# Other cuts of the expert weights and of the token rows in a routed mixture-of-experts stage

## Chip, cores, metric

One core of a Trainium2 chip. The metric is the device time of one execution in microseconds (us): 216.65 us before, the median of three (216.4 to 217.42). The profile is of one further execution with a span of 217.2 us. Times below without another source count from the start of that span.

## What is computed

An mLSTM attention cell for 4 x 8 heads, 768 steps and 40 columns gives 3,072 rows of 320 columns. A router sends each row to one of eight experts. The reference, cut to the part that the change touches:

```
logits = x @ w_gate                       # x: 3072 x 320
expert_idx = argmax(logits, axis=1)
for e in range(8):                        # rows sorted by expert
    h = maximum(x_sorted[lo:hi] @ w1[e], 0.0)     # w1[e]: 320 x 1024
    y_sorted[lo:hi] = h @ w2[e]                   # w2[e]: 1024 x 320
out = gate_w[:, None] * y_sorted[inv_perm]
```

## The kernel before

**Two stages.** Up to about 117 us the core works through 24 steps of 128 tokens: attention, then the router, then a scatter of each step's rows (`send`, L577) into a DRAM buffer sorted by expert. After that it runs the expert groups. The order on each engine is the program's order; nothing is rescheduled.

**Groups.** Each expert has three tiles of 128 rows at fixed places: a first group of two tiles and a second of one. I write (3,0) for the first group of expert 3 and (3,1) for its second. Experts 0 and 1 have their first groups done early, between the last router steps (L668 to L708). The rest run in the hand-written order L801: (2,0) (3,0) (0,1) (1,1) (4,0) (2,1) (5,0) (3,1) (4,1) (6,0) (5,1) (7,0) (6,1) (7,1). Five single tiles for experts with more than 384 rows follow. That makes 8 groups of two tiles and 13 of one, 29 tiles in all.

**One group.** `turn` (L230) transposes its rows on PE and copies the result to SBUF on DVE. The 320 columns are cut into 128, 128 and 64. The last piece is transposed twice, into partitions 0 to 63 and 64 to 127, so that two matmuls with 64 rows each can lie in the two halves of the PE array. `layer1` (L245) makes the 1,024 hidden columns in units: DVE applies the relu to the even ones (hidden columns 0 to 511), ACT to the odd ones. In a two-tile group there are four units. Units 0 and 2 each begin with four half matmuls (L258), followed by full ones (L267). In a one-tile group there are two units, and all eight half matmuls stand at the start. `layer2` (L277) multiplies by w2, ACT copies the result, and POOL scatters it to the output (L287). In PE's order the turn of the next group stands between `layer1` and `layer2` of the present one.

**Weights.** The weights lie in DRAM as 4-byte floats and are cast to 2 bytes on the way in, by DMAs that POOL issues: one of 256 rows for w1 (L178), two of 64 half rows (L183), and one for w2 (L189). An expert's weights are issued about three groups ahead. Every DMA from POOL takes the next of eight semaphores in turn and waits until the DMA eight before it has landed; POOL's later work waits behind it. L183 issues w1's last 64 rows: columns 0 to 511 to one half of the partitions, 512 to 1,023 to the other.

`warm` (L564) issues matmuls whose result nobody reads.

Of the kernel before, what the change touches and what calls it, by code (L numbers as in the profile page):

```python
# [8 lines left out]
F32 = mybir.dt.float32  # L9
BF16 = mybir.dt.bfloat16  # L10
# [9 lines left out]
def kernel(  # L20
# [13 lines left out]
    nc = tc.nc  # L34
    B, H, S, D = q.shape
    BH = B * H
    NB = S // 128
    N = B * S
    Dm = H * D
    E = moe_w_gate.shape[1]  # L40
    F = moe_w1.shape[2]
    FB = F // 128
    NT = N // 128
    PR = H // 2
    DP = 64
# [5 lines left out]
    dch = []  # L51
# [3 lines left out]
        d0 += 128  # L55
    DB = len(dch)

    FL = DB - 1
    HF = FB // 2
    wch = [d0 if dsz == 128 else Dm - 128 for d0, dsz in dch]  # L60
    assert NT * 128 == N and FB * 128 == F and D <= DP and dch[FL][1] == 64


    NJ = 3
# [5 lines left out]
    XW = 4  # L70
# [5 lines left out]
    ident_b = consts.tile([128, 128], BF16)  # L76
# [82 lines left out]
    xs = nc.dram_tensor("x_sorted", (E * NS, RW), BF16, kind="Internal").ap()  # L159

    big = ctx.enter_context(tc.tile_pool(name="big", bufs=1))
    w1_all = big.tile([128, E, FL * F + F // 2], BF16)
    w2_all = big.tile([128, E, FB, Dm], BF16)
    rte = ctx.enter_context(tc.tile_pool(name="rte", bufs=1))

# [9 lines left out]
    xg = [(x_all[:, NE * e : NE * (e + 1), :], x_all[:, NE * E + e : NE * E + e + 1, :]) for e in range(E)]  # L175

    def weights_in(e, n=1):
        nc.gpsimd.dma_start(  # L178
            w1_all[:, e, : FL * F].rearrange("p (a f) -> p a f", f=F),
            moe_w1[e, : FL * 128, :].rearrange("(a p) f -> p a f", p=128),  # L180
        )
        for i in range(2):
            nc.gpsimd.dma_start(  # L183
                w1_all[64 * i : 64 * i + 64, e, FL * F :], moe_w1[e, FL * 128 :, i * HF * 128 : (i + 1) * HF * 128],
            )

    def weights_out(e0, n):
        e = slice(e0, e0 + n)
        nc.gpsimd.dma_start(  # L189
            w2_all[:, e].rearrange("p e a d -> p (e a) d"), moe_w2[e].rearrange("e (a p) d -> p (e a) d", p=128),  # L190
        )

    def apart(ins, group):
# [24 lines left out]
    def spot(kind, shape, dtype):  # L218
        i = turns[kind] = turns.get(kind, -1) + 1
        at = spots[kind][i % len(spots[kind])]  # L220
        if isinstance(at, tuple):
            tag, pool = at
            return pool.tile(shape, dtype, name=kind, tag=tag)[:]
        n = 1
        for m in shape[1:]:
            n *= m
        at = at[:, :n]
        return at.rearrange("p (a b) -> p a b", b=shape[2]) if len(shape) == 3 else at

    def turn(g):  # L230
        n = g["n"]
        src = g["xg"] if "xg" in g else xg[g["e"]][g["k"]]
        g["xT"] = spot("xT", [128, DB, n * 128], BF16)
        tp = spot("tp", [128, DB, n * 128], BF16)
        for j in range(n):
            for db in range(DB):
                at = src[:, j, db * 128 : min(Dm, (db + 1) * 128)]
                if db < FL:
                    nc.tensor.transpose(tp[:, db, j * 128 : (j + 1) * 128], at, ident_b[:])
                    continue  # L240
                for r in range(2):
                    nc.tensor.transpose(tp[64 * r : 64 * r + 64, db, j * 128 : (j + 1) * 128], at, ident_b[:])
        nc.vector.tensor_copy(g["xT"], tp)

    def layer1(g, u):  # L245
        n = g["n"]
        per = 4 // n
        w, xT = g["w"][0], g["xT"]
        v = u // 2 * per
        if u == 0:  # L250
            g["h"] = spot("h", [128, FB, n * 128], BF16)
        if u % 2 == 0:
            g["hp"] = [spot("hp", [128, per, n * 128], F32) for _ in range(2)]
            for i in range(per):
                for a in range(2):
                    c = FL * F + (v + i) * 128
                    r = slice(64 * a, 64 * a + 64)
                    nc.tensor.matmul(  # L258
                        g["hp"][a][:, i, :], lhsT=w[r, c : c + 128], rhs=xT[r, FL, :], start=(i == 0), stop=False,
                        skip_group_check=True,  # L260
                    )
        a = u % 2
        hp = g["hp"][a]
        for i in range(per):
            for db in range(FL):
                c = db * F + (a * HF + v + i) * 128
                nc.tensor.matmul(  # L267
                    hp[:, i, :], lhsT=w[:, c : c + 128], rhs=xT[:, db, :], start=False, stop=(db == FL - 1),
                    skip_group_check=True,
                )  # L270
        dst = g["h"][:, a * HF + v : a * HF + v + per, :]
        if a == 0:
            nc.vector.tensor_relu(dst, hp)  # L273
        else:
            nc.scalar.activation(dst, hp, AF.Relu)  # L275
# [23 lines left out]
    def router():  # L299
        nc.vector.tensor_scalar_mul(wg_sb[:], wg_sb[:], -1.0)  # L300
# [6 lines left out]
    with tc.tile_pool(name="ring", bufs=1) as ring_pool, \  # L307
# [256 lines left out]
        def warm(n):  # L564
            j = ps1.tile([128, 512], F32, name="junk", tag="tk")
            for _ in range(n):
                nc.tensor.matmul(
                    j[:], lhsT=ident_b[:], rhs=st[NT - 1]["dA"][:].rearrange("p j t -> p (j t)"), start=True, stop=True,
                )

        def keep_rows(t):
            P = team_of[t]
            nc.scalar.activation(
                x_all[:, t, :Dm], st[t]["x"][:], AF.Copy, scale=rt[P]["gs"][:, t - teams[P][0] : t - teams[P][0] + 1],
            )
# [31 lines left out]
        for s in range(-3, NT):  # L607
            P, odd = (s - 4) // 2, s % 2
            last = s == NT - 1
            do(scores, s + 1)  # L610
            do(transposes, s + 2)
            if s == -3:
                masks()
            if s == -2:
                gates()
                router()
            do(values, s + 2)
            if odd and s > E and sent <= (s - 5 if s > 2 * PE_ + 4 else s - 6):
                send(sent)
                sent += 1  # L620
            if s == NT - 5:
                weights_in(0, 1)
            pair = not odd and 0 <= P
            if pair:
                gate(P)
            do(states, s)
            do(load, s + 6 if s >= -1 else -1)
            if pair:
                rank(P, s - 1)
            if last:  # L630
                warm(3)
            do(xtrans, s - 1)
            do(ogate, s + 2)
            do(attend, s)
            if pair:
                place(P)
                if P == PE_:
                    even_out(s - 1)
            if s == 2 * PE_ + 4:
                keep_rows(s - 4)  # L640
                keep_rows(s - 3)
            elif s != 2 * PE_ + 5:
# [27 lines left out]
            hp=[(t_, ps1) for t_ in ("sA", "sB", "tk", "tq")], tp=[("dC", ps1)],  # L670
            h=[kq[:, i].rearrange("p a h d -> p (a h d)").bitcast(BF16) for i in range(2)],
            xT=[kq[:, 2, a].rearrange("p h d -> p (h d)").bitcast(BF16) for a in range(2)],
# [4 lines left out]
        first, second = early  # L677
        targets(0, 0)
        turn(first)
        warm(2)  # L680
        xtrans(NT - 1)
        layer1(first, 0)
        logits(P0 + 1, NT)
# [74 lines left out]
    wk_pool = ctx.enter_context(tc.tile_pool(name="moe_wk", bufs=2))  # L758
# [24 lines left out]
        g["to"] = t[:, 0:1]  # L783

    def fetch(ex):
        wx1 = wk_pool.tile([128, FL * F + F // 2], BF16, name="wx1", bufs=XW)
        wx2 = wk_pool.tile([128, FB, Dm], BF16, name="wx2", bufs=XW)
        nc.sync.dma_start(wx1[:], w1_all[:, bass.ds(ex, 1), :].rearrange("p e b -> p (e b)"))
        nc.sync.dma_start(wx2[:].rearrange("p a b -> p (a b)"), w2_all[:, bass.ds(ex, 1)].rearrange("p e a b -> p (e a b)"))
        return wx1, wx2  # L790
# [47 lines left out]
    with tc.If(nx > XU):  # L838
        with tc.For_i(XU, nx, 1) as i:
            iv = wk_pool.tile([128, 1], F32, name="iv")  # L840
            nc.vector.tensor_copy(iv[:], invx[:, bass.ds(i, 1)])
            g = dict(n=1, w=fetch(expert_of(i)), apart=False)
# [36 lines left out]
```

## Time and profile before

| What | Value |
|---|---|
| PE busy, 145 to 167 us | 21.95 of 22 us |
| DMA engines' mean share, 117 to 178 us | 1.14 to 1.25 (transfers overlap on an engine) |
| POOL, eight weight sets: L178, L183 (each), L189 | 784, 585, 936 ns medians |
| One packet of w1, 2,048 bytes written (4,096 read) | 173 ns |
| One packet of w1, 1,024 bytes written | 96 ns |
| One packet of w2, 640 bytes written | 69 ns |

The last three rows are medians over the trace's packet records of POOL's DMA queue, where one packet is one contiguous run: 2,048, 1,024 and 8,192 packets of these sizes for eight experts. They also tell when an expert's weights were through (us from the span's start; the semaphore follows within a microsecond):

| Expert | w1 issued (POOL) | first w1 packet | last w1 packet | w1 first used | last w2 packet | w2 first used |
|---|---|---|---|---|---|---|
| 1 | 111.9 | 116.1 | 122.1 | 128.05 | 125.6 | 130.5 |
| 2 | 118.7 | 124.0 | 128.9 | 134.7 | 132.2 | 138.0 |
| 3 | 131.2 | 132.7 | 138.8 | 140.3 | 144.3 | 144.9 |
| 4 | 137.1 | 142.2 | 148.7 | 153.3 | 152.0 | 156.2 |
| 5 | 146.5 | 150.8 | 156.2 | 161.6 | 160.6 | 164.5 |
| 6 | 154.2 | 158.6 | 165.1 | 173.1 | 168.4 | 176.0 |
| 7 | 166.7 | 168.6 | 174.2 | 184.8 | 177.9 | 187.7 |

In the timeline, each line has its start, its length, the engine and source line, the operation with destination and source, a count, and in brackets how long the engine was idle before it and what ended that.

### The profile page before, as it was taken

Reading aid. Unit: us, or ns where it says so; the run is one execution under the profiler, and the core shown is the slowest. Engines: PE = TensorE matmul, PEld = TensorE weight load, DVE = VectorE, ACT = ScalarE, POOL = GpSimd, SP = SyncE. Lnnn points to the kernel's source line nnn. Section 1 sums busy time; section 2 is a strip of 40 time slices with the busy share of each in tenths; the row PEclk is TensorE's granted clock in tenths of the full one; section 3 lists DMA queues with packets and bytes.
Section 4 is the critical chain, followed back from the end, with each engine's and each line's share of the span. In section 5 each row is a group of like instructions: output and inputs, shape, how many; then the busy total and the mean of one; then the engine's idle time right before and its main releaser. Section 6 shows DMA issues by size and latency. Waiting matters only on the chain.

```text
span 217.2 us, 5727 instructions
## 1 busy us (share of the span) xinstructions
PE 192.3 (89%) x2048; PEld 151.8 (70%) x2057; DVE 124.8 (57%) x410; ACT 117.3 (54%) x273; POOL 139.3 (64%) x238
## 2 busy tenths in 40 slices
PE   1299999999999999979899998969999986999970
PEld 1168788899998899978786755647667654676740
DVE  7746667677787878797776342345833332333320
ACT  2458657797789897896751552323333322332330
POOL 6036786644869889749999489838656786253221
PEclk9999999999999999999998899999999999999996
DMA  7999999989999989994799999999999999985310
GB/s 139 197 198 190 205 205 204 231 156 254 178 193 173 195 161 206 193 204 84 142 184 262 222 205 150 193 254 233 216 229 245 231 290 408 409 317 201 149 46 10
DMA packets 120782, 44.32 MB, mean 204 GB/s; under 512 B 102506, under 2 KB 115821, under 8 KB 120752
## 3 DMA queue, kind: packets, MB, share of 16 engines
q1 hardware_dynamic: 105456, 25.34, 55.9%
q0 software_dynamic: 14832, 18.38, 40.3%
q8 instruction: 17, 0.28, 0.5%
q10 hardware_dynamic: 464, 0.21, 0.4%
q14 instruction: 13, 0.11, 0.2%
HBM read 39.30 MB, written 9.37 MB: 224 GB/s over the span
## 4 chain that ended last, share of the span: by engine, by line
PE 46%; POOL 20%; issue 14%; DVE 9%; DMA 5%; ACT 3%; POOLq 1%; ACTq 0%; DVEq 0%
POOL out_dram L287 7%; PE hp L474 6%; PE zp L280 5%; DMA w_all<-in_moe_w_dram 5%; PE hp L406 5%; PE tk L368 4%; POOL x_sorted L579 4%; PE dC L414 4%; PE hp L267 4%; PE tq L368 3%; PE xt L451 3%; PE sA L386 3%; PE sA L381 2%; POOL x_sb L444 2%; POOL rest L297 2%
## 5 line engine op out<-in xcount | busy, mean ns | idle before, releaser
L273 DVE TENSOR_SCALAR h<-hp 128x512 bf16<-128x512 f32 x25 | 17.3, 692 | 40.6 <-PE hp L267 26.3
L287 POOL DMA_INDIRECT out_dram<-zo,s_idx x20 | 20.0, 1002 | 16.3 <-ACT zo L285 10.0
L275 ACT ACTIVATE h<-hp 128x512 bf16<-128x512 f32 x25 | 14.9, 597 | 25.2 <-PE hp L267 19.9
L579 POOL DMA_INDIRECT x_sorted<-x_all,slots x24 | 25.3, 1054 | 4.9 <-issue 3.9
L444 POOL TENSOR_TENSOR x_sb<-x_sb,den 128x320 f32<-128x320 f32 x23 | 16.8, 729 | 17.2 <-DVE den L442 17.1
L280 PE MATMUL zp<-w_all,h 128*128 128x320 bf16 x160 | 24.5, 300 | 3.5 <-DMA w_all<-in_moe_w_dram 1.6
L280 PEld LDWEIGHTS <-h 128*128 128x128 bf16 x200 | 17.7, 98 | 13.2 <-DVE h L273 2.7
L285 ACT COPY zo<-zp 128x320 f32<-128x320 f32 x25 | 10.7, 426 | 27.2 <-PE zp L280 23.7
L267 PEld LDWEIGHTS <-w_all 128*128 128x128 bf16 x256 | 18.4, 98 | 5.6 <-issue 3.4
L393 ACT CAST dB<-sB 128x512 bf16<-128x512 f32 x24 | 14.0, 585 | 13.7 <-PE sB L387 11.5
L267 PE MATMUL hp<-xT,w_all 128*128 128x128 bf16 (+1 forms) x224 | 21.1, 243 | 0.0
L406 PE MATMUL hp<-C_sb,qT 104*128 104x82 f32 x160 | 20.7, 272 | 0.0
L368 PE MATMUL tk<-ident,kq 128*104 128x128 f32 x96 | 16.4, 296 | 4.2 <-DMA kq<-in_k_dram 4.2
L406 PEld LDWEIGHTS hp<-C_sb,qT 104*128 104x128 f32 x160 | 19.4, 192 | 0.3
L453 ACT COPY xT<-xt 128x384 f32<-128x384 f32 x24 | 11.6, 482 | 13.5 <-PE xt L451 12.5
L356 POOL CAST vAb<-vA 128x328 bf16<-128x328 f32 x24 | 11.0, 459 | 11.7 <-DVE vA L354 11.7
L474 PE MATMUL hp<-wg_sb,xT 128*128 128x8 f32 x144 | 18.0, 258 | 0.0
L414 PE MATMUL dC<-vA,kq 128*104 128x82 f32 x160 | 17.9, 254 | 0.0
L394 POOL TENSOR_SCALAR_AFFINE_SELECT dB<-dB 128x512 bf16<-128x512 bf16 x24 | 16.5, 689 | 1.7 <-ACT dB L393 1.5
L474 PEld LDWEIGHTS hp<-wg_sb,xT 128*128 128x128 f32 x144 | 17.4, 195 | 0.1
L391 DVE TENSOR_TENSOR dA<-sA,cmask 128x512 bf16<-128x512 f32 x24 | 16.0, 669 | 1.4 <-PE sB L387 1.4
L414 PEld LDWEIGHTS dC<-vA,kq 128*104 128x104 f32 x160 | 16.3, 172 | 0.0
(160 smaller groups left out, 455.8 us busy)
## 6 DMA issues: line engine op xcount, KB each, us to landing
wx<-w_all SPq DMA_DIRECT2D x10, 640.0 KB
w_all<-in_moe_w_dram POOLq DMA_DIRECT2D x8, 640.0 KB
w_all<-in_moe_w_dram POOLq DMA_DIRECT2D x8, 512.0 KB
kq<-in_k_dram SPq DMA_DIRECT2D x24, 160.0 KB
kq<-in_q_dram SPq DMA_DIRECT2D x24, 160.0 KB
v<-in_v_dram SPq DMA_DIRECT2D x24, 160.0 KB
o_sb<-in_o_gate_dram SPq DMA_DIRECT2D x24, 160.0 KB
x_sorted<-zrow POOLq DMA_DIRECT2D x8, 241.5 KB
```

Of the source, the lines that this page charges most:

```text
L267: nc.tensor.matmul(hp[:, i, :], lhsT=w[:, c : c + 128], rhs=xT[:, db, :], start=False, stop=(db == FL - 1), skip_group_check=True,)
L273: nc.vector.tensor_relu(dst, hp)
L280: nc.tensor.matmul(zp, lhsT=g["h"][:, fb, j * 128 : (j + 1) * 128], rhs=g["w"][1][:, fb, :], start=(fb == 0), stop=(fb == FB - 1),)
L287: ins = nc.gpsimd.indirect_dma_start(out=out[:, :], out_offset=bass.IndirectOffsetOnAxis(ap=at, axis=0), in_=zo, in_offset=None, bounds_ch ...
L368: nc.tensor.transpose(tp[:, j, :], two(d[n], j), ident[:])
L391: nc.vector.tensor_tensor(d["dA"][:], sA[:], cmask[:, None, :].to_broadcast([128, PR, 128]), op=ALU.mult)
L394: nc.gpsimd.affine_select(d["dB"][:], d["dB"][:], compare_op=ALU.is_ge, fill=0.0, base=0, pattern=[[0, PR], [1, 128]], channel_multiplier=-1,)
L406: nc.tensor.matmul(hp[:, 2 * j * D1 : (2 * j + 2) * D1], lhsT=d["qT"][:, j, :], rhs=st["C"][:, j].rearrange("p h d -> p (h d)"), start=(j ...
L414: nc.tensor.matmul(st["dC"][:, j], lhsT=two(d["k"], j), rhs=d["vA"][:, 2 * j : 2 * j + 2, :], start=(c == 0 and j == 0), stop=True, skip_g ...
L444: eng.tensor_tensor(x3d, x3d, den[:].unsqueeze(2).to_broadcast([128, H, D]), op=ALU.mult)
L474: nc.tensor.matmul(lg[:, i * E : (i + 1) * E], lhsT=st[t]["xT"][:, db * 128 : (db + 1) * 128], rhs=wg_sb[:, db, :], start=(fresh and i == ...
L579: ins = nc.gpsimd.indirect_dma_start(out=xs[:, :], out_offset=bass.IndirectOffsetOnAxis(ap=slots[:, t : t + 1], axis=0), in_=x_all[:, t, : ...
```

## The change

The 320 columns are cut into pieces that overlap: columns 0 to 127, 64 to 191, and 192 to 319. Three full transposes then give all that is needed: piece 0 holds columns 64 to 127 in its upper partitions, piece 1 the same columns in its lower ones. So one of the two 64-row halves is read from piece 1, the other from piece 0, and the two transposes of 64 columns are not needed. Hidden columns of even units take piece 0 and piece 2 in full and the other 64 columns as a half matmul; those of odd units take piece 1 and piece 2. To suit, w1's DMAs are cut anew: 128 rows of 4,096 bytes, 128 x 2 half rows, and 128 half rows.

All half matmuls of a group now stand ahead of its full ones, so a two-tile group opens four PSUM tiles at its start. In w2, two neighbouring rows go to one partition, for runs of 2,560 bytes in DRAM; the hidden columns are permuted to match, which makes the weight slices of `layer1` step over every second column. Two calls of `warm` issue two matmuls more each.

```
     def weights_in(e, n=1):
+        half = F // 2
+        at = moe_w1.offset + e * Dm * F
+        nc.gpsimd.dma_start(w1_all[:, e, :F], moe_w1[e, parts[2] : parts[2] + 128, :])
         nc.gpsimd.dma_start(
-            w1_all[:, e, : FL * F].rearrange("p (a f) -> p a f", f=F),
-            moe_w1[e, : FL * 128, :].rearrange("(a p) f -> p a f", p=128),
-        )
-        for i in range(2):
-            nc.gpsimd.dma_start(
-                w1_all[64 * i : 64 * i + 64, e, FL * F :], moe_w1[e, FL * 128 :, i * HF * 128 : (i + 1) * HF * 128],
-            )
+            w1_all[:, e, F : 2 * F].rearrange("p (a f) -> p a f", a=2),
+            bass.AP(moe_w1.tensor, at, [[F, 128], [64 * F + half, 2], [1, half]]),
+        )
+        nc.gpsimd.dma_start(
+            w1_all[:, e, 2 * F :],
+            bass.AP(moe_w1.tensor, at + half, [[128 * F - half, 2], [F, 64], [1, half]]),
+        )
...
         nc.gpsimd.dma_start(
-            w2_all[:, e].rearrange("p e a d -> p (e a) d"), moe_w2[e].rearrange("e (a p) d -> p (e a) d", p=128),
+            w2_all[:, e].rearrange("p e (a j) d -> p (e a) (j d)", j=2),
+            moe_w2[e].rearrange("e (a p j) d -> p (e a) (j d)", p=128, j=2),
         )
...
-                at = src[:, j, db * 128 : min(Dm, (db + 1) * 128)]
-                if db < FL:
-                    nc.tensor.transpose(tp[:, db, j * 128 : (j + 1) * 128], at, ident_b[:])
-                    continue
-                for r in range(2):
-                    nc.tensor.transpose(tp[64 * r : 64 * r + 64, db, j * 128 : (j + 1) * 128], at, ident_b[:])
+                nc.tensor.transpose(tp[:, db, j * 128 : (j + 1) * 128], src[:, j, parts[db] : parts[db] + 128], ident_b[:])
...
+    def column(fb):
+        return fb // 2 * 256 + fb % 2
...
-        if u % 2 == 0:
-            g["hp"] = [spot("hp", [128, per, n * 128], F32) for _ in range(2)]
-            for i in range(per):
+            g["hp"] = [spot("hp", [128, per, n * 128], F32) for _ in range(2 * n)]
+            for k in range(HF):
                 for a in range(2):
-                    c = FL * F + (v + i) * 128
-                    r = slice(64 * a, 64 * a + 64)
+                    c = 2 * F + column(k)
+                    r = slice(64 - 64 * a, 128 - 64 * a)
                     nc.tensor.matmul(
-                        g["hp"][a][:, i, :], lhsT=w[r, c : c + 128], rhs=xT[r, FL, :], start=(i == 0), stop=False,
-                        skip_group_check=True,
+                        g["hp"][k // per * 2 + a][:, k % per, :], lhsT=w[r, c : c + 255 : 2], rhs=xT[r, 1 - a, :],
+                        start=(k % per == 0), stop=False, skip_group_check=True,
                     )
...
-            for db in range(FL):
-                c = db * F + (a * HF + v + i) * 128
+            fb = a * HF + v + i
+            for c, db in ((F + column(fb), a), (column(fb), 2)):
                 nc.tensor.matmul(
-                    hp[:, i, :], lhsT=w[:, c : c + 128], rhs=xT[:, db, :], start=False, stop=(db == FL - 1),
+                    hp[:, i, :], lhsT=w[:, c : c + 255 : 2], rhs=xT[:, db, :], start=False, stop=(db == 2),
...
             if last:
-                warm(3)
+                warm(5)
...
         turn(first)
-        warm(2)
+        warm(4)
         xtrans(NT - 1)
```

More of the change, by code (lines that the diff above doesn't have):

```diff
@@ L56 @@
     DB = len(dch)
-    FL = DB - 1
     HF = FB // 2
     wch = [d0 if dsz == 128 else Dm - 128 for d0, dsz in dch]
-    assert NT * 128 == N and FB * 128 == F and D <= DP and dch[FL][1] == 64
+    assert NT * 128 == N and FB * 128 == F and D <= DP and Dm == 5 * 64
+    parts = [0, 64, 192]
     NJ = 3
@@ L161 @@
     big = ctx.enter_context(tc.tile_pool(name="big", bufs=1))
-    w1_all = big.tile([128, E, FL * F + F // 2], BF16)
+    w1_all = big.tile([128, E, 5 * F // 2], BF16)
     w2_all = big.tile([128, E, FB, Dm], BF16)
@@ L251, in layer1 @@
             g["h"] = spot("h", [128, FB, n * 128], BF16)
-        if u % 2 == 0:
-            g["hp"] = [spot("hp", [128, per, n * 128], F32) for _ in range(2)]
-            for i in range(per):
+            g["hp"] = [spot("hp", [128, per, n * 128], F32) for _ in range(2 * n)]
+            for k in range(HF):
                 for a in range(2):
-                    c = FL * F + (v + i) * 128
-                    r = slice(64 * a, 64 * a + 64)
+                    c = 2 * F + column(k)
+                    r = slice(64 - 64 * a, 128 - 64 * a)
                     nc.tensor.matmul(
-                        g["hp"][a][:, i, :], lhsT=w[r, c : c + 128], rhs=xT[r, FL, :], start=(i == 0), stop=False,
-                        skip_group_check=True,
+                        g["hp"][k // per * 2 + a][:, k % per, :], lhsT=w[r, c : c + 255 : 2], rhs=xT[r, 1 - a, :],
+                        start=(k % per == 0), stop=False, skip_group_check=True,
                     )
         a = u % 2
-        hp = g["hp"][a]
+        hp = g["hp"][u]
         for i in range(per):
-            for db in range(FL):
-                c = db * F + (a * HF + v + i) * 128
+            fb = a * HF + v + i
+            for c, db in ((F + column(fb), a), (column(fb), 2)):
                 nc.tensor.matmul(
-                    hp[:, i, :], lhsT=w[:, c : c + 128], rhs=xT[:, db, :], start=False, stop=(db == FL - 1),
+                    hp[:, i, :], lhsT=w[:, c : c + 255 : 2], rhs=xT[:, db, :], start=False, stop=(db == 2),
                     skip_group_check=True,
@@ L785, in fetch @@
     def fetch(ex):
-        wx1 = wk_pool.tile([128, FL * F + F // 2], BF16, name="wx1", bufs=XW)
+        wx1 = wk_pool.tile([128, 5 * F // 2], BF16, name="wx1", bufs=XW)
         wx2 = wk_pool.tile([128, FB, Dm], BF16, name="wx2", bufs=XW)
```

## Prediction

> **What bounds the kernel now.** I read the page's busy shares first, then the busy time by stretch, then the timeline of the expert groups, and last the packet records. The attention stage (to about 117 us) is touched by nothing but two spare matmuls. For the expert stage the stretches say which engine is full:
>
> ```profile
> 134.00:145.00 11.00, 8.67 (x78) 5.73 (x79) 5.24 (x13) 3.24 (x6) 7.02 (x9) 1.00 1.17 212
> 145.00:156.00 11.00, 10.95 (x120) 7.52 (x118) 5.89 (x19) 3.52 (x8) 7.82 (x10) 1.00 1.22 225
> 156.00:167.00 11.00, 11.00 (x111) 7.38 (x110) 4.77 (x15) 4.15 (x9) 6.39 (x8) 1.00 1.25 223
> ```
>
> The columns are length, PE, weight load, DVE, ACT, POOL, clock, DMA share, GB/s. From 145 us PE has no gap; before it there are some, and the DMA engines are full in all three. Where weights are late, the timeline says so:
>
> ```profile
> 122.12 0.53 POOL L183 DMA_DIRECT2D w_all<-in_moe_w_dram  x1 [2.11 <-DMA w_all<-in_moe_w_dram]
> ...
> 133.01 0.99 POOL L189 DMA_DIRECT2D w_all<-in_moe_w_dram  x1
> ...
> 144.86 2.33 PE L280 MATMUL zp<-w_all,h 128*128 128x320 bf16 x16 [1.64 <-DMA w_all<-in_moe_w_dram]
> 145.52 1.03 POOL L287 DMA_INDIRECT out_dram<-zo_e,s_idx  x1 [3.28 <-DMA w_all<-in_moe_w_dram]
> ```
>
> PE waits 1.64 us for w2 of expert 3, issued at 133.01. So up to 144.86 the end is set by expert 3's weights, and what PE saves earlier is lost in that wait. Later experts have 3 to 10 us in hand (table). POOL twice waits for a landing before it may issue.
>
> The price of transposes and of switching is read from one group, (2,1), with the turn of (5,0):
>
> ```profile
> 158.44 0.40 PE L258 MATMUL hp<-xT,w_all 64*128 64x128 bf16 x8
> 158.77 1.07 PE L267 MATMUL hp<-xT,w_all 128*128 128x128 bf16 x16
> 159.50 0.69 DVE L273 TENSOR_SCALAR h<-hp 128x512 bf16<-128x512 f32 x1 [1.75 <-PE hp L267]
> 159.67 0.28 PE L239 MATMUL tp<-ident_b,x_all 128*128 128x128 bf16 x2
> 159.88 0.25 PE L242 MATMUL tp<-ident_b,x_all 128*64 128x128 bf16 x2
> 160.05 0.29 PE L239 MATMUL tp<-ident_b,x_all 128*128 128x128 bf16 x2
> 160.27 0.25 PE L242 MATMUL tp<-ident_b,x_all 128*64 128x128 bf16 x2
> 160.45 1.26 PE L280 MATMUL zp<-w_all,h 128*128 128x320 bf16 x8
> ```
>
> Starts count, not durations. Sixteen full matmuls take 159.67 - 158.77 = 0.90, 0.056 each. Eight half matmuls lie in pairs, 4 x 0.056 = 0.22, but take 0.33: 0.11 is the change of shape. A tile's transposes take (160.45 - 159.67) / 2 = 0.39: three columns' worth, 0.17, and two changes of shape, 0.22.
>
> [...] No weight load of before is strided[...]; the packed ones hide behind matmuls 0.056 apart. [...]
>
> **The change part by part.**
>
> *Transposes.* Three full ones take 3 x 0.056 = 0.17 in place of 0.39: 0.22 saved per tile on PE. In a one-tile group layer2 must also wait for the first relu: 159.50 + 0.69 = 160.19, plus 0.06 to start. Before a turn of one tile nothing is gained there, since layer2 waits for DVE already; before a turn of two tiles 0.20 (160.45 to 160.25) of the 0.44.
>
> *Half matmuls first.* A two-tile group changes shape at two places rather than four: 0.22 saved in each. One-tile groups have this order already. In expert 1's early group the fourth PSUM tile is the one that ACT copies out until 128.59, while half matmuls start at 128.05: some 0.3 lost, one copy.
>
> *Sum on PE.* Before expert 3's layer2: 0.44 (turn of (2,0)), 0.66 in (2,0) (turn of (3,0) and halves), 0.22 in (3,0), less 0.1 in the early group: 1.2 us, all ahead of the weight wait. After it: two-tile groups (4,0), (5,0), (6,0), (7,0), each 0.22 and one tile's turn, 4 x 0.44; one-tile groups ahead of a two-tile turn, (1,1), (2,1), (4,1), (5,1), 4 x 0.20; the rest 0. **2.6 us** that reach the end. The last five single tiles keep their 2.99 us period, the relu being in the chain.
>
> *Spare matmuls.* In `warm(5)` two more, 0.43, fall into PE's idle 0.65 ahead of L451; `warm(4)` takes up the 0.44 that the turn ahead of it gives back. Zero; at most a better clock around 120 us (granted 0.90 from 117 to 134), under 0.5.
>
> *w2's runs.* A line through 69, 96 and 173 ns gives 19 ns + 0.075 ns per byte written, so a 1,280-byte packet 115 ns: estimate. 512 x 115 = 58.9 engine-us per expert for 1,024 x 69 = 70.7: 3.7 us per engine rather than 4.4. w1 goes from 256 x 173 + 128 x 96 = 56.6 to 128 x 173 + 384 x 96 = 59.0. POOL's issue: the same four DMAs.
>
> *Where w1's third piece runs.* Its DRAM side counts [2][64][512]; its SBUF side counts 128 partitions. [...] two engines carry 64 packets each, 64 x 96 ns = **6.1 us**, where 16 engines would take 0.8. This is the disputed cost, 0 to 5.4 us, and I take the upper end[...]. Such a pair then has per expert 8 x 0.173 + 16 x 0.096 + 6.14 = 9.1 us of w1 and 3.7 of w2, 12.8 in all, where every engine of before has 2.8 + 0.8 + 4.4 = 8.0. I expect another pair for each expert, so no engine is overloaded in total; but a weight set is there when its slowest engine is.
>
> *Following it.* Expert 1: first packet 116.1, third piece through at 125.2 to 128 rather than 122.1. The scatter of L579 at 124.47 is eight DMAs behind it and waits; the three scatters and expert 3's issue queue up on POOL. The third scatter (128.02) is eight behind w2 of expert 1, through at 129 to 132. So expert 3's weights are issued 1 to 3 us later. Expert 2's w1 is through by 133 to 134 and used at about 134: just in time. Expert 3: w1 came at full rate from 134, now from about 136, plus 9.1 us times 1.0 to 1.2 for the other traffic (before, 8.0 us of work took 10.3): **145 to 147** for a first use at about 139.5. PE idles 5 to 7 us. Then w2 on the same pair, 3.7 us: 148.5 to 151, where it was 144.3; layer1 of (3,0) fits between. I take 149: layer2 of (3,0) starts 4.2 us later than at 144.86. From there on the table's 4 us and more in hand cover the later experts, since PE is late too.
>
> **Forecast (A).** 216.65 + 4.2 - 2.6 = **218.3 us**. With the smallest delay (overlapping packets, +1.8) 215.8; with the largest (+6.5) 220.6.
>
> **Rivals.** *B: the third piece is spread over 16 engines.* For: nothing in the profile of before shows a narrow DMA. Then w2 of expert 3 comes about 0.5 us earlier (0.7 less w2, 0.15 more w1), and the end moves by 0.5 + 2.6: 213.6. *C: strided weight loads are slow.* If a load takes twice the matmul's 0.056, one-tile groups pay: 13 x 16 x 0.056 = 11.6 on full matmuls, less some 3 that waits for relu hide: about 225. Against: [...] 98 ns load records that overlap today. *D: delay and gain cancel*, PE's idle being filled by DMA engines that serve the lone pair faster: 216.6. PE's stalls of about 4 us from 176 to 183.6 ("issue") may also shift by 1 us either way.
>
> **Chances.** A 0.55 as a band from 215.8 to 221 (about a quarter of it below 215.6 to 216, a half above 217.7), B 0.30, C 0.06, D 0.09. Faster by over 0.5%: 0.28 of B and 0.13 of A, 0.41. Within: 0.13. Slower: 0.46. The range runs from B to A's upper end, 213.2 to 221.3; C and the tails are left out.
>
> **What would show it.** Right: packets of 1,024 bytes that end for each expert some 4 us after its others, with two at a time in flight at the end; PE waiting for a DMA at the first half matmuls of (3,0) for several us; POOL's scatters at 124 to 130 waiting for weight DMAs; the transposes of a tile 0.17 us apart; full matmuls of one-tile groups still 0.056 apart. Wrong: the third piece through with the rest, and POOL's timetable unmoved (B); one-tile `layer1` longer than 1.24 us (C).

## The result and the profile after

| | before | after |
|---|---|---|
| Median of four runs, us | 216.53 (215.6 to 217.42) | 222.67 (222.14 to 224.66) |
| Ratio | | 1.030, 95% interval 1.022 to 1.038 |
| Profiled execution, us (span) | 218.99 (217.2) | 223.08 (221.3) |
| layer2 of (3,0) starts | 144.86 | 153.11 |
| from there to the last scatter | 66.93 | 61.60 |
| from the last scatter to the end | 5.4 | 6.6 |

Slower, by 6.1 us. Some executions of a kernel take 1.5% or more longer than its fastest; ratios here leave those out, medians do not. The profiled execution of before, at 218.99 us, lay above all four in the median; this matters below. The three lower rows add up to the difference of the spans: 8.25 - 5.33 + 1.2 = 4.1.

Read the timeline of the changed kernel first:

```profile
128.90 1.03 POOL L580 DMA_INDIRECT x_sorted<-x_all,slots  x1 [5.79 <-ACT zo_e L286]
...
135.68 0.60 POOL L180 DMA_DIRECT2D w_all<-in_moe_w_dram  x1
...
148.78 1.03 PE L259 MATMUL hp<-xT,w_all 64*128 64x256 bf16 x8 [8.50 <-DMA w_all<-in_moe_w_dram]
149.56 1.06 POOL L288 DMA_INDIRECT out_dram<-zo_e,s_idx  x1 [4.74 <-DMA w_all<-in_moe_w_dram]
...
153.11 2.33 PE L281 MATMUL zp<-w_all,h 128*128 128x320 bf16 x16 [0.40 <-DMA w_all<-in_moe_w_dram]
```

PE stands for 8.50 us in front of the first half matmuls of (3,0). The scatter of 124.47 comes at 128.90. The trace names an ACT copy for its 5.79 us; that copy is not what ended the wait, as the experiment with only expert 1's piece narrow shows. The trace also records when a DMA's semaphore is raised, 16 times for each of these three, and these increments show both waits directly:

| Changed kernel | issued | 14 increments by | the last two | what waits for them starts |
|---|---|---|---|---|
| expert 1, third piece | 114.44 | 124.50 | 127.39, 128.07 | scatter, 128.90 |
| expert 3, third piece | 136.97 | 142.65 | 148.63, 148.74 | half matmuls of (3,0), 148.78 |
| expert 3, w2 | 137.93 | 146.97 | 152.91, 152.97 | layer2 of (3,0), 153.11 |

By stretch:

```profile
134.00:145.00 11.00, 5.45 (x54) 4.04 (x51) 2.56 (x5) 2.47 (x5) 10.14 (x15) 0.99 0.94 150
145.00:156.00 11.00, 6.81 (x57) 4.63 (x58) 2.62 (x8) 2.04 (x4) 3.83 (x5) 0.70 1.06 221
156.00:167.00 11.00, 10.75 (x124) 7.84 (x122) 7.39 (x26) 4.09 (x8) 7.46 (x10) 1.00 1.13 184
```

In the first two rows PE was busy 7.4 us less than before, 12.3 us of 22. The DMA share of the first row fell from 1.17 to 0.94: a mean over 16 engines does not show two that work for longer. The PE work itself became cheaper as planned; here are (2,1), the turn of (5,0), then (5,0):

```profile
158.31 0.40 PE L259 MATMUL hp<-xT,w_all 64*128 64x128 bf16 x8
158.64 1.07 PE L268 MATMUL hp<-xT,w_all 128*128 128x128 bf16 x16
...
159.54 0.50 PE L241 MATMUL tp<-ident_b,x_all 128*128 128x128 bf16 x6
...
160.12 1.26 PE L281 MATMUL zp<-w_all,h 128*128 128x320 bf16 x8
...
161.31 0.61 PE L259 MATMUL hp<-xT,w_all 64*128 64x256 bf16 x8
161.85 1.92 PE L268 MATMUL hp<-xT,w_all 128*128 128x256 bf16 x16
...
163.61 0.33 PE L241 MATMUL tp<-ident_b,x_all 128*128 128x128 bf16 x3
163.78 2.42 PE L281 MATMUL zp<-w_all,h 128*128 128x320 bf16 x16
```

A tile's transposes take 163.78 - 163.61 = 0.17 us. Sixteen full matmuls with weight slices that step over every second column take 159.54 - 158.64 = 0.90, as before. The narrow DMA has a signature on the page. Before, then after, from the second and third parts:

```profile
DMA packets 120782, 44.32 MB, mean 204 GB/s; under 512 B 102506, under 2 KB 115821, under 8 KB 120752
...
q0 software_dynamic: 14832, 18.38, 40.3%
```

```profile
DMA packets 124877, 44.33 MB, mean 200 GB/s; under 512 B 109674, under 2 KB 120941, under 8 KB 124848
...
q0 software_dynamic: 18928, 18.41, 40.8%
```

Same bytes, but 7,168 more packets under 512 bytes. In the packet records they are of 4 bytes and on POOL's queue (q0): 7,168 = 8 experts x 14 x 64. The number fits fourteen engines that carry nothing of a third piece and have 64 packets of 4 bytes each for it, while two carry 64 real ones; the packet records do not name the engine. For expert 3 these small packets are through by 142.3, while its real ones go on to about 148.2.

### The profile page after: what moved, and what is told of

It reads as the page before. It is cut to its first block, busy times and chain, and to the rows that moved or that the text cites. A ratio compares the mean times of both kernels' runs of the same rounds, so it can differ in the third digit from the quotient of the medians.

```text
span 221.3 us, 5677 instructions
## 1 busy us (share of the span) xinstructions
PE 187.7 (85%) x2023; PEld 152.5 (69%) x2032; DVE 123.6 (56%) x410; ACT 117.2 (53%) x273; POOL 140.7 (64%) x238
## 3 DMA queue, kind: packets, MB, share of 16 engines
q0 software_dynamic: 18928, 18.41, 40.8%
## 4 chain that ended last, share of the span: by engine, by line
PE 39%; DMA 21%; POOL 16%; DVE 8%; issue 8%; ACT 4%; SPq 1%; POOLq 0%; ACTq 0%; DVEq 0%
DMA w_all<-in_moe_w_dram 18%; PE hp L407 5%; PE hp L475 5%; PE tk L369 4%; POOL x_sorted L580 4%; PE zp L281 4%; PE dC L415 4%; POOL out_dram L288 4%; PE tq L369 3%; PE sA L387 3%; PE sA L382 3%; DMA wx<-w_all 3%; PE xt L452 3%; PE hp L268 2%; POOL x_sb L445 2%
## 5 line engine op out<-in xcount | busy, mean ns | idle before, releaser
L268 PEld LDWEIGHTS <-w_all 128*128 128x128 bf16 x256 | 19.4, 100 | 4.4 <-issue 1.9
```

The costliest lines, as they stand in the source:

```text
L268: nc.tensor.matmul(hp[:, i, :], lhsT=w[:, c : c + 255 : 2], rhs=xT[:, db, :], start=False, stop=(db == 2), skip_group_check=True,)
```

## The experiments

Five sets of kernels, each set on one chip; the third and fourth were on the same one. Before's medians there were 220.38 (the first four kernels), 223.99 (the next four), 216.86, 216.80 (four each) and 222.88 (the last two). Times are compared within a set.

**How many engines the third piece uses.** The DRAM side of that one DMA, in four versions. Two of them read other rows of w1 than the layer needs, but as many bytes; their output is not the layer's:

```
 changed:        [[128 * F - half, 2], [F, 64], [1, half]]
 four engines:   [[33 * F, 4], [F, 32], [1, half]]            # other rows of w1
 wide:           [[F, 128], [1, half]]                        # other rows of w1
 two halves:     two DMAs of 64 rows, the reference's rows
```

> The changed kernel with the third DMA's DRAM side counting 4 first, over other rows of w1 than the computation asks for, the same 128 x 2,048 bytes. Theory (engines in use follow the first count): 32 packets of 96 ns on each of four engines, 3.1 us rather than 6.1; the delay of expert 3 is between that of two engines and of sixteen: the time is 215 to 218.5 us. Rival: as with two, 221 to 223 us, or as with sixteen, 213 to 214.5 us, if engines don't follow that count.

> The changed kernel with one edit: the third DMA of w1 reads 128 rows one step apart (other rows of w1 than the computation asks for, the same 128 x 2,048 bytes), so that both of its access patterns count 128 first. Theory (third piece on two engines): the lone pair is gone; packets of 1,024 bytes end with the rest, POOL's scatter at 124 us no longer waits for a weight DMA, PE's wait of 8.5 us at the half matmuls of group (3,0) falls under 1.5 us, and the time is 213 to 214.5 us. Rival (the finer cut of w1, the four PSUM tiles opened at once or the strided weight loads cost the time): the DMA is as fine as ever, so it stays at 221 to 223 us.

> The changed kernel with w1's third piece as two DMAs of 64 rows each, as L183 had it; five DMAs per expert rather than four. Theory: 213 to 215 us, like the 128-row read, plus at most 0.6 us of POOL's issue per expert, of which only expert 3's is on the path, and a wait on the eighth DMA before that comes one DMA sooner. Rival (another part of the change costs the time): 221 to 223 us.

Four engines, in PE's timeline:

```profile
143.25 0.61 PE L259 MATMUL hp<-xT,w_all 64*128 64x256 bf16 x8 [2.90 <-DMA w_all<-in_moe_w_dram]
147.66 2.33 PE L281 MATMUL zp<-w_all,h 128*128 128x320 bf16 x16 [1.77 <-DMA w_all<-in_moe_w_dram]
```

| leading count of the third piece | 2 | 4 | 128 |
|---|---|---|---|
| packets under 512 B, more than the wide kernel's 102,506 | 7,168 = 8 x 14 x 64 | 3,072 = 8 x 12 x 32 | 0 |
| wait for weights at (3,0)'s half matmuls, us | 8.50 | 2.90 | none |
| layer2 of (3,0) starts | 153.11 | 147.66 | 143.57 |

The packet counts fit two and four engines exactly, and the wait follows. The semaphore records agree: with four engines, expert 1's third piece has twelve increments by 123.44 and four from 124.86 to 125.59. But the times missed: wide took 220.22 us (217.89 to 221.41), two halves 223.45 (219.18 to 223.62), against 220.38 (219.37 to 225.95), too scattered for a ratio; four engines 223.9, ratio 1.017 (1.013 to 1.021). The profile of the wide kernel says where its gain went, in DVE's and ACT's lines of (5,1):

```profile
179.90 0.69 DVE L274 TENSOR_SCALAR h<-hp 128x512 bf16<-128x512 f32 x1 [5.13 <-issue]
...
183.81 0.60 ACT L276 ACTIVATE h<-hp 128x512 bf16<-128x512 f32 x1 [6.56 <-remote]
```

Both engines stand still though PE's work for them is long done; PE lost 5.5 us there. PE's granted clock was then 0.50 from 181.3 to 188.1, so that layer1 of (7,0) took 3.3 us where (5,0) of the changed kernel takes 2.3. The two halves lost 6.0 us of PE in the same way, four engines 5.6. Before has such a standstill at the same group (DVE 4.54 us, PE some 3.5), the changed kernel has none.

**The same fault put into the kernel before**: its two DMAs of 64 rows merged into one whose DRAM side counts 2 first.

```
-        for i in range(2):
-            nc.gpsimd.dma_start(
-                w1_all[64 * i : 64 * i + 64, e, FL * F :], moe_w1[e, FL * 128 :, i * HF * 128 : (i + 1) * HF * 128],
-            )
+        nc.gpsimd.dma_start(
+            w1_all[:, e, FL * F :],
+            bass.AP(moe_w1.tensor, moe_w1.offset + e * Dm * F + FL * 128 * F, [[F // 2, 2], [F, 64], [1, F // 2]]),
+        )
```

> The kernel before with one edit: its two DMAs of 64 half rows become one whose DRAM side counts 2 first (three DMAs per expert rather than four, the same bytes in the same places). Theory: each expert's w1 ends on two engines with 64 packets of 96 ns each; group (3,0) waits some 6 to 10 us, the time is 221 to 226 us, with none of PE's gains. Rival (the narrow DMA is hidden): 215.5 to 217.5 us.

231.65 us, ratio 1.054 (1.049 to 1.059): one DMA fewer per expert, the same bytes, and 11 us more, above what was expected. Against before's own profile 5.9 us of it are there at layer2 of (3,0) and 1.4 at the end; where the rest goes was not followed. The narrow DMA cost as much without the new layout.

```profile
145.17 0.39 PE L258 MATMUL hp<-xT,w_all 64*128 64x256 bf16 x4 [2.02 <-DMA w_all<-in_moe_w_dram]
...
150.73 4.01 PE L280 MATMUL zp<-w_all,h 128*128 128x320 bf16 x16 [2.60 <-DMA w_all<-in_moe_w_dram]
```

**Is the standstill the work of the weight copies** for the last five tiles, which run at that time? Without them (the tiles use expert 0's weights, so their output is not the layer's), in the kernels before, changed and wide; and once with the copies kept but issued later, from ACT's queue, on top of the two halves:

```
-            groups[len(order) + x]["w"] = fetch(expert_of(x))
+            groups[len(order) + x]["w"] = (w1_all[:, 0, :], w2_all[:, 0])
```

> The kernel before without the ten copies of expert weights within SBUF for the last five single tiles, which use expert 0's weights instead (their rows come out as expert 0 would have them). Question: PE, DVE and ACT all stand still for 3 to 6 us between 175 and 188 us in each run of before and of the wide versions, just when these copies begin, and not in the changed kernel, whose copies begin 13 us later. Theory (the copies cause the standstill): it is gone, and the time falls by 3 to 5 us against before. Rival (it belongs to the scatters or to the last weights): under 1 us.

> The changed kernel without the ten copies of weights for the last five single tiles (they use expert 0's weights). Theory: in the changed kernel the copies already lay behind the groups that they disturb, so it falls by less than 1.5 us; against the kernel before without copies it is 5.5 to 7 us slower (8.3 us later at layer2 of group (3,0), less 2.6). Rival (the copies cost both the same): it falls as much as before does.

> The changed kernel with the 128-row read of other rows of w1 as third piece, and without the ten copies (the last five tiles use expert 0's weights). Theory (narrow DMA costs, the rest of the change gains, the copies hide it): 2.5 to 4 us faster than the kernel before without copies, and 8 to 10 us faster than the changed kernel without copies. Rival (PE's part of the change gains nothing): as fast as the kernel before without copies.

> The changed kernel with the third piece as two DMAs of 64 rows, and with the ten copies issued from ACT's queue in ACT's order, three groups ahead of their use, so that they begin near 185 us rather than 176. Theory (two things cost: the lone engine pair, and copies that begin among the groups): no standstill, 4 to 7 us faster than with the copies from SP, 2 to 5 us faster than the kernel before. Rival: the standstill moves along with the copies, and nothing is gained.

The late copies:

```
-        nc.sync.dma_start(wx1[:], w1_all[:, bass.ds(ex, 1), :].rearrange("p e b -> p (e b)"))
+        eng.dma_start(wx1[:], w1_all[:, bass.ds(ex, 1), :].rearrange("p e b -> p (e b)"))   # eng: ACT's queue; wx2 alike
...
-        x = i - len(order) + XW
+        x = i - len(order) + 3
```

Before without copies took 224.81 us (220.48 to 226.62) and still had the standstill, 3.9 us on PE; wide without copies had it too (PE 3.5 and 1.4). So it does not need the copies. Late copies took 225.74, ratio 1.012 (1.003 to 1.021): a miss. The pair changed and wide without copies gave 229.80 and 220.14: 9.7 us for the number of engines alone, and the wide one at 0.984 (0.976 to 0.992) of before with its copies.

**The delay in two parts.** Only expert 1's third piece narrow, or only expert 3's; the others as in the wide kernel, which ran again beside them. A fourth kernel had neither the copies nor the weights of experts 6 and 7 to carry.

```
-            bass.AP(moe_w1.tensor, at + half, [[128 * F - half, 2], [F, 64], [1, half]]),
+            bass.AP(moe_w1.tensor, at + half, [[128 * F - half, 2], [F, 64], [1, half]]) if e == 1
+            else bass.AP(moe_w1.tensor, at, [[F, 128], [1, half]]),
```

The other edits: `e == 3` in its place; and for the fourth kernel

```
-        if g.get("k") == 0 and nw < E:
+        if g.get("k") == 0 and nw < 6:            # groups of experts 6 and 7 take the weights of 5
```

> The changed kernel with w1's third piece as 128 rows one step apart (other rows of w1 than the reference's, same bytes), a second time, as the common reference for the next three. All theories: third scatter-stage wait on POOL at about 124.5 us, expert 3's weights issued at 131.3, layer2 of (3,0) at 143.6 to 145.5 without a wait of more than 2 us for weights, a standstill of 4 to 6 us of PE at (5,1), 0.975 to 1.00 of the kernel before.

> As the one before, but expert 1's third piece alone counts 2 first (its rows are the reference's; the other experts' are other rows). Theory (the delay has two parts, this one being POOL's: the scatter that is eight DMAs behind expert 1's third piece waits, and everything behind it on POOL comes later): the scatter at 128 to 129 in place of 124.6, expert 3's weights issued at 134.5 to 136 rather than 131.3, layer2 of (3,0) 3 to 4.5 us later than in the wide kernel, at 147 to 149, the whole 3 to 4 us slower than the wide kernel. Rival (only the narrow piece of the expert in use matters, since expert 1's weights have 2 us and more in hand): issue moves, but PE at (3,0) waits under 1 us and the end stays within 1 us of the wide kernel's.

> Expert 3's third piece alone counts 2 first. Theory (direct part): POOL's timetable as in the wide kernel (scatter 124.6, issue 131.3), PE waits 3 to 5 us at the first half matmuls of (3,0), layer2 of (3,0) at 147 to 149, 3 to 5 us slower than the wide kernel; the two parts sum to the changed kernel's 8 to 9.7 us. Rival (the pair is overloaded only because every expert's narrow piece falls on a few engines in succession): a single narrow piece costs under 2 us at (3,0).

> The wide kernel without the five weight copies between SBUF buffers (the last five tiles use expert 0's weights) and without loading experts 6 and 7 (their groups use expert 5's weights), so that the DMA engines carry little after about 163 us. On the standstill of DVE and ACT at (5,1), 4 to 6 us of PE in the wide kernel: if it needs full DMA engines, PE's gaps between 170 and 190 us fall under 1 us and the whole is 4 to 6 us faster than the wide kernel, 0.955 to 0.975 of the kernel before. If it belongs to the place in the program whatever the DMA engines do, 3 us or more remain at (5,1) and the time is within 1.5 us of the wide kernel's.

Expert 1 narrow, then expert 3 narrow:

```profile
127.50 1.02 POOL L580 DMA_INDIRECT x_sorted<-x_all,slots  x1 [4.12 <-DVE kq L242]
...
141.27 0.61 PE L259 MATMUL hp<-xT,w_all 64*128 64x256 bf16 x8 [1.67 <-DMA w_all<-in_moe_w_dram]
...
146.28 3.36 PE L281 MATMUL zp<-w_all,h 128*128 128x320 bf16 x16 [1.16 <-DMA w_all<-in_moe_w_dram]
```

```profile
125.06 1.02 POOL L580 DMA_INDIRECT x_sorted<-x_all,slots  x1 [1.22 <-ACT x_all L574]
...
145.48 1.03 PE L259 MATMUL hp<-xT,w_all 64*128 64x256 bf16 x8 [5.45 <-DMA w_all<-in_moe_w_dram]
149.81 2.33 PE L281 MATMUL zp<-w_all,h 128*128 128x320 bf16 x16 [0.32 <-DVE s_idx L215]
```

| | wide | expert 1 narrow | expert 3 narrow |
|---|---|---|---|
| time, us | 211.29 | 213.52 | 217.38 |
| ratio to before (interval) | 0.975 (0.967 to 0.982) | 0.983 (0.974 to 0.991) | 1.008 (1.005 to 1.011) |
| scatter on POOL | 124.73 | 127.50 | 125.06 |
| expert 3's w1 issued | 131.52 | 134.26 | 131.91 |
| layer2 of (3,0) | 144.14 | 146.28 | 149.81 |

With expert 1's piece narrow alone the scatter waits, and 4.12 us of it are put down to a DVE copy that the wide kernel has as well, without such a wait; the piece's last two increments came at 126.23 and 126.67, 0.83 us ahead of the scatter. With expert 3's piece narrow alone its last two came at 145.42 and 145.43, and those of its w2 at 149.63 and 149.68, just ahead of layer2. So POOL's part (2.1 us at layer2, 2.2 in the end) and the direct part (5.7, 6.1) are separate. At layer2 they add up to 7.8, near the 7.4 by which the changed kernel lies behind the wide one in the next set. In time they make 8.3 of 11.2; of the rest, 1.6 us stand behind the last scatter, and the remainder was not split. Each part missed the expected figure: the first was smaller, the second larger. On this chip none of the four profiles has the standstill, with the weights of experts 6 and 7 and the copies or without, so the fourth kernel told nothing of it. Its 218.02 us (ratio 1.008, 1.005 to 1.011) are odd: its profile has 11 us between the last scatter and the end, and I have no cause for them. The wide kernel is the same program as in the first set: a span of 217.4 there, 209.6 here. So the standstill is not the program's alone; the chip or the execution has a part in it.

**Changed and repaired beside each other.** The changed kernel, the wide one, the two halves, and the halves of all eight experts fetched early, by two DMAs at expert 0's place:

```
+        if e == 0:
+            for i in range(2):
+                nc.gpsimd.dma_start(
+                    w1_all[64 * i : 64 * i + 64, :, 2 * F :],
+                    moe_w1[:, 128 * i : 128 * i + 64, (1 - i) * half : (2 - i) * half].rearrange("e p f -> p e f"),
+                )
```

> The changed kernel once more, beside the three that follow, since chips and executions differ by whether DVE and ACT stand still at (5,1). Theory (the loss against the kernel before is the late weights of expert 3, 8 to 9 us, less 3 to 4 us of cheaper PE work behind it): 2 to 3.5% slower than before, layer2 of (3,0) at 152 to 154. Rival (the loss on record came from one chip's state): within 1% of before.

> The kernel with 128 rows one step apart (other rows of w1), on this chip. Theory: 8 to 10 us faster than the changed kernel, 0.965 to 0.985 of before where no standstill is seen, and about 1.0 where one is. Rival: as far from the changed kernel as call one's medians would say, some 2 us.

> The third piece as two DMAs of 64 rows with the reference's rows, five DMAs per expert. Theory (narrowness is gone, but five DMAs per expert turn the eight semaphores faster, so that the scatter at 127 waits and expert 3's weights are issued at 133.6 rather than 131.3): layer2 of (3,0) at 145 to 147, 5 to 7 us faster than the changed kernel, 0.98 to 1.00 of before. Rival (a fifth DMA costs nothing): equal to the wide kernel within 1 us.

> The reference's rows again, but the third pieces of all eight experts loaded by two DMAs of 64 rows x 8 experts at expert 0's place in the attention stage, so that each expert has three DMAs in the expert stage and 128 x 96 ns = 12.3 engine-us less to carry. Theory: no wait at the first half matmuls of (3,0), scatter at 124 to 125, layer2 of (3,0) at 142 to 145, as fast as the wide kernel or up to 2 us faster, 0.96 to 0.985 of before. Rival (1,024 packets at about 102 us delay the attention stage's loads or expert 0's own weights): the attention stage ends 1 us or more later and the gain is lost, 0.985 to 1.00.

| | time, us | ratio to before (interval) | layer2 of (3,0) |
|---|---|---|---|
| changed | 224.14 | 1.035 (1.030 to 1.041) | 151.63 |
| wide | 212.97 | 0.980 (0.973 to 0.987) | 144.27 |
| two halves | 212.62 | 0.980 (0.975 to 0.985) | 145.95 |
| early halves | 212.94 (210.03 to 216.55) | 0.982 (0.977 to 0.987) | 143.86 |

The two halves compute what the reference does, and on this chip turn 3.5% slower into 2% faster: **11.5 us** for one DMA cut in two. All 16 increments of both halves of expert 3 were there by 140.18. Their fifth DMA per expert does delay expert 3's issue (132.95, against 131.39 in the wide kernel) and layer2 by 1.7 us, but the wide kernel lost as much at once, its layer2 of (3,0) taking 4.01 us rather than 2.33 while its clock was 0.50 (144.3 to 147.7). The early halves have the earliest layer2 and no better time; whether they gain stays open.

**What the end follows.** From the last scatter to the end, these profiles but for the odd one above follow the number of packets on POOL's queue once it is over some 12,000: before and the four-engine kernel both have 14,832, and both 5.4 us. Two kernels change that number through w2's runs alone: the two halves with w2 as before, and the kernel before with the long runs.

```
-            w2_all[:, e].rearrange("p e a d -> p (e a) d"), moe_w2[e].rearrange("e (a p) d -> p (e a) d", p=128),
+            w2_all[:, e].rearrange("p e (a j) d -> p (e a) (j d)", j=2),
+            moe_w2[e].rearrange("e (a p j) d -> p (e a) (j d)", p=128, j=2),
```

> The third piece as two DMAs of 64 rows, and w2 as in the kernel before (1,280-byte runs in DRAM, contiguous weight slices): what the longer w2 runs are worth. In all profiles so far but one the time from the last scatter to the end follows the number of packet records on POOL's queue: 3.7 to 4.0 us at 11,700, 4.4 at 12,656, 5.4 at 14,832, 6.6 at 18,928, 6.85 at 21,872. Theory (the packets set that time): 4,096 records more than with long runs, 15,984 in all, so 5.5 to 6.0 us from the last scatter to the end rather than 3.8; and w2 of expert 3 some 0.7 us later; together 2 to 3 us slower than with long runs, 0.985 to 1.00 of before. Rival (the end belongs to the kind of the last DMAs, not to the packets): 3.8 us at the end, under 1 us slower.

> The kernel before with one part of the change alone: w2 in 2,560-byte runs and the weight slices of layer1 stepping over every second column. Theory: 10,736 records on POOL's queue, 3.5 to 4.0 us from the last scatter to the end rather than 5.4, layer2 of (3,0) 0.5 to 1 us earlier, full matmuls of one-tile groups still 0.056 us apart; 2 to 2.5 us faster than before, 0.985 to 0.993 of it. Rival: 5.4 us at the end, at most 0.7 us faster.

The last scatters of the two halves and of the two halves with short runs, spans 210.9 and 219.1:

```profile
207.16 0.98 POOL L289 DMA_INDIRECT out_dram<-zo,si  x1 [2.00 <-ACT zo L287]
```

```profile
213.41 0.98 POOL L288 DMA_INDIRECT out_dram<-zo,si  x1 [2.00 <-ACT zo L286]
```

| packets on q0 | 10,736 | 11,888 | 14,832 | 15,984 | 18,928 |
|---|---|---|---|---|---|
| kernel | before, long runs | two halves | before | two halves, short runs | changed |
| last scatter to end, us | 4.1 | 3.8 | 5.4 | 5.7 | 6.6 |

With short runs the two halves have 4,096 packets more and 1.9 us more there, in a stretch of which the records show nothing after the first 2 us; the kernel before gains 1.3 us by the long ones. Below 12,000 packets the order is lost. In time, short runs left 221.00 us (ratio 0.989, 0.974 to 1.004), and long runs alone brought before to 221.40 (0.991, 0.986 to 0.996), both ratios as expected. In the latter layer2 of (3,0) came at 144.82, no earlier than before; the trace puts its wait down to DVE.

## Why the prediction was wrong

The direction and the mechanism were right: two engines for the third piece (the small packets and the late increments fit two), the scatter of L579 waiting, expert 3's weights late, PE idle at the first half matmuls of (3,0). The forecast of 218.3 us, and its range up to 221.3, fell short of 222.67. Four terms of the sum:

- **The delay, 4.2 us predicted, was 8.25.** This is the step that failed, in three places. *The issue:* expert 3 was issued 4.5 us later (131.19 to 135.68), not 1 to 3, and its first packet came at 137.0 rather than 136: 1.0 us. Expert 1's third piece was through at 128.07, just past the 125.2 to 128 of the prediction, and the scatter began another 0.83 us later. *"9.1 us times 1.0 to 1.2":* w1 took 11.8 us to PE's start at 148.78, where 10.0 was the middle: 1.8 us. The packets took to about 148.2, which is 11.2 us or 9.1 x 1.23. The factor of 1.2 was below the one that the prediction had itself read in before, 10.3 us for 8.0 of work, or 1.29. The half microsecond from the last packet to the semaphore (148.2 to 148.74) was not in the sum. The price of a packet was not the fault. From 141.3 to 143.8 the piece's packets began at 25 per us, more than the 2 / 0.096 = 21 of two engines at the predicted price. From 144 to 147 they came at 13 to 18 per us. By then the loads of token rows from SP's queue ran at 93 to 139 packets of 644 bytes per us; that the pair shared its time with them is my reading. *w2:* layer2 began 4.3 us after PE's start, where 3 was left for it, less than the 3.7 at which w2 on the pair was priced: 1.3 us. Its last increments came 4.2 us after those of the third piece.
- **The gain behind it, 2.6 us predicted.** The single savings hold. A two-tile group with a turn of one tile takes 163.78 - 161.31 = 2.47 us, against 2.90 in before (173.08 to 175.98): 0.43, predicted 0.44. A one-tile group ahead of a two-tile turn takes 1.48 from the full matmuls to layer2 against 1.68: 0.20, as predicted. Up to layer2 of (6,0) 1.8 us arrived of the 1.9 predicted by then. The 0.44 of (7,0) was lost: its layer2 waited for its own w2, though the prediction took later experts to be covered. The 5.33 us of the profiles contain before's standstill of some 3.5.

```profile
190.71 2.33 PE L281 MATMUL zp<-w_all,h 128*128 128x320 bf16 x16 [0.33 <-DMA w_all<-in_moe_w_dram]
```

- **The end, not in the sum at all**: 1.2 us more. The 4-byte packets raised the number on POOL's queue by 7,168, while w2's longer runs lowered it by 4,096 and w1's cut raised it by 1,024. Without the narrow DMA the longer runs gain here: 3.8 against 5.4.
- **The starting point.** The prediction added to the median of 216.65 what it read from a profile of an execution of 218.99. "Stalls of about 4 us from 176 to 183.6" were named, with "1 us either way"; they were 3.5 us. From 218.99 to 223.08 is 4.1, as the table's rows say; from median to median 6.1. The difference would be explained if the median execution had only some 1.5 us of these stalls (8.25 - 1.8 + 1.2 - 1.5 = 6.1), but none like it was traced.

Right as well: about two packets of 1,024 bytes in flight at the end (1.7 to 2.5 from 142 to 147), 1,280-byte packets at 116 ns (estimated 115), the strided weight slices free at 0.056 us a matmul (rival C falls), the last five tiles at 2.99 us each. Rival B, 16 engines, fell for this kernel. Its 213.6 us is nearly what the two halves take beside a kernel before of 216.80, 212.62; that is luck, since the terms behind it differ. Rival D fell too: nothing filled the gap.

That a leading count of 2 puts the piece on two engines was an assumption of mine: no DMA in the profile of before showed it. The runs fit it, and four engines at a count of 4: 14 x 64 and 12 x 32 more packets of 4 bytes per expert, and two and four semaphore increments that come late. At 128 there is neither a packet more nor a wait for weights at (3,0)'s half matmuls. By my reading the pair changed from expert 1 to expert 2: in the changed kernel expert 2's second piece has two late increments (133.47, 134.11; the others by 130.07), but its third piece four (133.25 to 134.54; the others by 130.47), so it did not fall on the pair that was still behind.

## What to carry to other kernels

Before a transfer goes into a kernel whose weights are just in time, read the slowest count of its DRAM side: here one DMA that counted 2 first had its last increment 6.1 us after its fourteenth (expert 3), and cutting it in two by partitions was worth 11.5 us on one chip; on another the standstill hid the gain. Price a late transfer by what its slowest engine must carry besides it (here 9.1 us were priced for the pair, 6.1 of them for the piece, and the packets took 11.2), and follow it twice: directly to its user (5.7 us at layer2 of (3,0)), and through the semaphores to whatever the issuing queue does eight DMAs later (2.1 us there). Add gains read from a profile to the time of the execution that was profiled, not to a median of others.

## What the runs showed of the hardware

- The changed kernel, whose third piece counts 2 first, has 896 more packets of 4 bytes per expert than the kernel before; with 4 first there are 384 more. This fits 64 for each of 14 engines and 32 for each of 12. In the changed kernel they raise the page's count of packets under 512 bytes from 102,506 to 109,674.
- Of the third piece's 16 semaphore increments in the changed kernel, the last came 3.6 us (expert 1: 124.50 to 128.07) and 6.1 us (expert 3: 142.65 to 148.74) after the fourteenth.
- Expert 3's narrow piece began 25 packets of 1,024 bytes per us from 141.3 to 143.8, each recorded at 98 ns. If two engines carried them, that is one every 79 ns on each, less than the recorded length.
- From the last scatter to the end the two halves took 3.8 us with 11,888 packets on POOL's queue and, with w2's short runs, 5.7 us with 15,984. What happens in that stretch, the records do not show.
- DVE and ACT stood still for 4 to 8 us at (5,1), always the same place, in before's profile and in most of those from chips where before took 220 us and more; in others of those, shorter stalls lay in several groups. None of the eight profiles of the third and fourth sets, which ran on one chip, has it. Leaving out the copies did not remove it. In six profiles where PE lost 3.9 us or more to it, the clock then was 0.50 for 6.8 us. Its cause is open.
- In the changed kernel PE's clock was granted 0.50 from 144.7 to 151.6, beginning 4.4 us into a gap of PE from 140.3 to 148.78, and the first sixteen full matmuls of (3,0) took 2.79 us, where (5,0)'s took 1.92. In the fourth set the two halves waited 2.85 us ahead of layer2 and kept 1.00; the wide kernel waited 2.04 us and was granted 0.50 from 144.3 to 147.7. What decides it was not found.
